# A pre-LN block on one core: weight readiness moved behind the store, weight sums stored sooner, a third fold buffer, and query exponentials stored from the activation engine

## The chip, the cores and the metric

The kernel runs on 1 core of one Trainium2 chip, with all five instruction queues of that core in use: TensorE (PE), VectorE (DVE), ScalarE (ACT), GpSimd (POOL) and the sync engine (SP), which here does nothing but issue DMAs. The metric is device time of one launch in microseconds (us). The kernel before takes 1948.48 us, the median of 3 runs (1946.75 to 1950.21).

## The reference, cut to what matters

One sequence of 2048 tokens, width 1024, 32 heads of 32, feed-forward width 3584, all float32:

```python
h  = x + A(layernorm(x), wqkv, w_phi, wo)
h2 = h + relu(layernorm(h) @ w1) @ w2

def A(x, wqkv, w_phi, wo):
    q, k, v = heads(x @ wqkv)
    pq, pk = q @ w_phi, k @ w_phi                       # per head, 32 x 32
    phi_q = concat(softmax(pq), softmax(-pq))           # 64 features
    phi_k = concat(softmax(pk), softmax(-pk))
    kv, z = phi_k.T @ v, phi_k.sum(over tokens)
    return (phi_q @ kv) / (phi_q @ z + 1e-6) @ wo
```

## The kernel before, in words

Every large product is made of three TensorE passes: both operands are split into a high part and a low part, and `mm3` (lines 180 to 183) issues high x high, high x low and low x high. ACT makes the high part of a weight (line 124), POOL or DVE subtracts to get the low part (line 128).

The work is a list of items. Items 0 to 31 project keys and values of the first 8 token tiles (4 column slices of 8 items), 32 to 47 their queries, 48 to 95 the same for the other 8 tiles; then come attention and the output product, the up projection, the down projection. An item of a projection has 8 steps, each three matmuls with 512 columns. Everything beside it is hung on a step by hand: `when(step, f, ...)` records `f` right after that step of the whole list. So each engine's queue is fixed before the run and is taken strictly in order.

Three kinds of side work matter here.

Folding. The key and query weights are multiplied with `w_phi` on the chip, in eight pieces p of eight blocks k each. `fold_step` issues four small matmuls into one of two PSUM banks named `tp` and copies them with ACT into a tile called `wp0` in the source and `wp` in the profile (lines 288 and 291); two blocks fill one tile. `fold_store` (line 300) has SP write the tile to DRAM (`wpk` for keys, `wpq` for queries) and, in the kernel before, marks the two blocks as usable at once. The weight ring `Units` asks `ready(key)` in every step and, when a block is marked and a raw buffer is free, records its load on SP (line 310 for the key half, 311 for the value half, 314 for a query block). Key slice 0 of the first half never goes through this; `ready` lets slice 0 pass always.

Weight sums. `t_load` has SP bring 512 KB of `w1` or `w2` into one of two tiles `b` (line 337), `t_sum` has POOL form four sums in place (line 347), `t_store` has SP write the result to DRAM (line 350, `t<-b`). There are 56 such rounds, one in ten steps, in the projections. A `t_load` can't start before the store of the round two earlier has landed, since it reuses that tile.

Query exponentials. For each of 32 query items DVE writes a tile `qe` (lines 502 and 503, two tiles in turn), ACT takes the exponential (line 507), and SP writes it to DRAM (line 511, `ed<-qe`), from where attention reads it later. The `when` lines for it are three steps after the exponential's.

```python
298        r = (p - 4) % 2
300        sp.dma_start(dst..., wp_of.pop((p, j))...)          # fold_store: then marks both blocks
1069   when(step + 9 + k, t_sum, j, k)
1070   when(step + 18, t_store, w, p, j)
```

Of the kernel before, what the change touches and what calls it, by code (L numbers as in the profile page):

```python
# [9 lines left out]
F32 = mybir.dt.float32  # L10
# [5 lines left out]
P = 128  # L16
# [123 lines left out]
def kernel(  # L140
# [12 lines left out]
    v, act, pool, pe, sp = nc.vector, nc.scalar, nc.gpsimd, nc.tensor, nc.sync  # L153
# [12 lines left out]
    def tp_bank():  # L166
        return psum.tile([P, 512], F32, name="tp", bufs=2)
# [20 lines left out]
    def do(n, k, f, *args):  # L188
        at[n, k].append((f, args))
# [6 lines left out]
    ed = [dram.tile([P, 8, 4, 256], F32, name=f"ed{b}") for b in range(4)]  # L196
# [65 lines left out]
    fp = folds.enter_context(tc.tile_pool(name="fold", bufs=2))  # L262
# [13 lines left out]
    def fold_mm(p, k, ps):  # L276
        for i in range(2):
            pe.matmul(ps[:, i * P:(i + 1) * P], wt_of[p, i][:, k * P:(k + 1) * P],
                      bd[:, (2 * p + i) % 8, :], start=True, stop=True)

    def fold_step(p, k):
        ps = tp_bank()[:, 0:256]
        fold_mm(p, k, ps)
        if k % 2 == 0:
            wp_of[p, k // 2] = fp.tile([P, 512], F32, name="wp0", bufs=2)
        sb = wp_of[p, k // 2][:, k % 2 * 256:(k % 2 + 1) * 256]
        if p < 4:
            act.activation(sb, ps, AF.Copy)
        else:

            act.activation(sb.rearrange("p (r c f) -> p c r f", r=2, c=4),
                           ps.rearrange("p (c r f) -> p c r f", r=2, c=4), AF.Copy)

    wp_of = {}

    def fold_store(p, j):

        r = (p - 4) % 2
        dst = wpk[p][2 * j:2 * j + 2] if p < 4 else wpq[(p - 4) // 2][2 * j:2 * j + 2, :, r * 256:(r + 1) * 256]
        sp.dma_start(dst.rearrange("k p f -> p k f"), wp_of.pop((p, j)).rearrange("p (k f) -> p k f", k=2))  # L300
        for k in (2 * j, 2 * j + 1):
            if p < 4 or p % 2:
                folded.add(("kv", p, k) if p < 4 else ("q", (p - 4) // 2, k))
# [83 lines left out]
        place[0] = k % 2 == 1  # L387

    def first_copy(j):
        wp_of[0, j] = fp.tile([P, 512], F32, name="wp0", bufs=2)  # L390
        act.activation(wp_of[0, j], first_ps.pop(j), AF.Copy)

    def ready(key):
# [10 lines left out]
    e_of, v_of, phi_of, kv_ps, kd_of = {}, {}, {}, {}, {}  # L404
# [100 lines left out]

    def q_second(s, t):
        act.activation(e_of[s, t], e_of[s, t], AF.Exp)

    def q_store(s, t):
        b, i = place_of[t]  # L510
        sp.dma_start(ed[b][:, 4 * s:4 * s + 4, i, :], e_of[s, t].rearrange("p (a c) s f -> p a (c s f)", a=4))

    def q_third(s, t):
        b, i = place_of[t]
# [312 lines left out]
    def item(gen, *args, keys):  # L827
        items.append((gen, args + (keys,)))
        steps.extend((k,) for k in keys)
        return len(items) - 1  # L830
# [11 lines left out]
    for b, tiles in enumerate(groups):  # L842
        for hf in range(2):

            pairs = b == 0 and hf == 0
            for j in range(0, 4, 2 if pairs else 1):
# [3 lines left out]
                for half in range(2):  # L850
                    n = item(wo_pair, tiles[j:j + 2], hf, half, keys=[("wo", hf, 4 * half + k // 2) for k in range(8)])
# [26 lines left out]
    def when(step, f, *args):  # L878

        if step < 8 * first_up:  # L880
            do(step // 8, step % 8, f, *args)
        else:
            do(first_up + (step - 8 * first_up) // 4, step % 4, f, *args)
# [4 lines left out]
    for t in range(1, NT):  # L888
        n = t - 1 if t < HT else q_n[1, t - HT] + 1
# [20 lines left out]
    for i, j in enumerate((2, 3, 0, 1)):  # L910
        do(1 + i // 2, 2 + 4 * (i % 2), first_copy, j)
        when(8 * (1 + i // 2) + 2 + 4 * (i % 2) + 3, fold_store, 0, j)
    todo = [(p, k) for p in range(1, 8) for k in range(NK)]
    for n in range(1, 32):
        for k in ((6,) if n < 8 and n not in (3, 4, 5) else (2, 6)):
            if not todo:
                break
            p, kk = todo.pop(0)
            do(n, k, fold_step, p, kk)
            if kk % 2:  # L920
                when(8 * n + k + 3, fold_store, p, kk // 2)
            if kk == 2 and p < 7:
                do(n, k, wt_load, p + 1, sp)
    assert not todo
# [71 lines left out]
    a0 = last_kv + 6  # L996
    for (sl, t), n in q_n.items():
        when(8 * n + 14, q_second, sl, t)
        when(8 * n + 17, q_store, sl, t)
        when(8 * n + 19, q_third, sl, t)  # L1000
    for u in range(32):
        start = 8 * (a0 + u) if u >= 8 else 8 * (last_kv + 4) + 19 * u // 2
# [32 lines left out]
    def up_step(b, p, m):  # L1035

        return up0 + 4 * (up_n[b, p, m] + 1 - first_up)

    for j, m in enumerate(UP):

        for g in range(2):
            step = up0 + (8 * j + (-62, -32)[g] if j < 4 else 6 * (j - 4) + 10 + 2 * g)
# [4 lines left out]
            step = up_step(0, NP - 1, m) + 3 * j  # L1047
# [13 lines left out]
    for n, (w, p, j) in enumerate((w, p, j) for w in (1, 2) for p in range(NP) for j in range(2)):  # L1061
        step = 24 + 10 * n
        if step > 8 * q_n[1, 0] - 20:
            step += 64
        when(step, t_load, w, p, j)
        for k in range(4):
            when(step + 9 + k, t_sum, j, k)
        when(step + 18, t_store, w, p, j)

    for b in range(2):  # L1070
        for m in DOWN:
            n = down_n[b, m, NP - 1] + 1
            name, more = {1: "x1", 5: "x4", 6: "x2", 4: "x3"}.get(m), \
# [111 lines left out]
```

## Time and profile before

| | us |
|---|---|
| median of 3 runs | 1948.48 |
| lowest, highest run | 1946.75, 1950.21 |
| the profiled execution's own time | 1954.31 |
| its span in the trace | 1952.5 |
| PE busy in the span | 1911.8 (98%) |
| DVE, POOL, ACT busy | 1027.3, 966.4, 756.0 |
| mean clock granted to PE | 0.993 of full |

The profile is one execution. PE's row of 40 slices reads 9 nearly everywhere; the slices that read lower are the first and the seventh (8) and the third (7). A matmul's busy time includes its pipelined tail, so a busy PE is an upper reading. The DMA row (mean busy share of 16 engines) runs from 5 to 8 tenths.

### The profile page before, as it was taken

Reading aid. Unit: us, or ns where it says so; the run is one execution under the profiler, and the core shown is the slowest. Engines: PE = TensorE matmul, PEld = TensorE weight load, DVE = VectorE, ACT = ScalarE, POOL = GpSimd, SP = SyncE. Lnnn points to the kernel's source line nnn. Section 1 sums busy time; section 2 is a strip of 40 time slices with the busy share of each in tenths; the row PEclk is TensorE's granted clock in tenths of the full one; section 3 lists DMA queues with packets and bytes.
Section 4 is the critical chain, followed back from the end, with each engine's and each line's share of the span. In section 5 each row is a group of like instructions: output and inputs, shape, how many; then the busy total and the mean of one; then the engine's idle time right before and its main releaser. Section 6 shows DMA issues by size and latency. Waiting matters only on the chain.

```text
span 1952.5 us, 31527 instructions
## 1 busy us (share of the span) xinstructions
PE 1911.8 (98%) x11416; PEld 1563.7 (80%) x11416; DVE 1027.3 (53%) x1695; ACT 756.0 (39%) x1374; POOL 966.4 (49%) x935
## 2 busy tenths in 40 slices
PE   8979998999999999999999999999999999999999
PEld 6867887877877777788888888888888888888887
DVE  5646567866759976645454464433443343334333
ACT  5422224422223312135454464444444444444442
POOL 3646672389984788622333322222244444444443
PEclk9999999999999999999999999999999999999999
DMA  5667777556657556788677796665677677876665
GB/s 189 202 219 251 254 248 245 175 183 218 204 190 232 176 192 207 251 273 250 220 247 245 255 309 215 203 196 182 196 248 227 202 220 229 261 216 214 216 215 178
DMA packets 292701, 432.16 MB, mean 221 GB/s; under 512 B 24384, under 2 KB 150336, under 8 KB 292544
## 3 DMA queue, kind: packets, MB, share of 16 engines
q1 hardware_dynamic: 292544, 430.14, 69.7%
q8 instruction: 90, 1.47, 0.3%
q14 instruction: 67, 0.55, 0.1%
HBM read 292.68 MB, written 137.36 MB: 220 GB/s over the span
## 4 chain that ended last, share of the span: by engine, by line
PE 77%; DMA 11%; POOL 6%; DVE 2%; issue 1%; SPq 1%; ACT 1%; POOLq 0%; ACTq 0%; DVEq 0%
PE mm L181 19%; PE mm L182 19%; PE mm L183 19%; DMA t<-b 5%; PE ac L183 4%; PE ac L182 4%; PE ac L181 4%; POOL b L347 3%; PE tp L183 2%; PE tp L181 2%; PE tp L182 2%; DMA b<-in_w_dram 2%; POOL w L128 2%; PE tp L244 1%; POOL zacc L437 1%
## 5 line engine op out<-in xcount | busy, mean ns | idle before, releaser
L128 POOL TENSOR_TENSOR w<-raw,w 128x512 fp32r<-128x512 f32 x355 | 472.6, 1333 | 736.1 <-ACT w L124 694.2
L124 ACT ACTIVATE w<-raw 128x512 fp32r<-128x512 f32 x686 | 408.8, 626 | 500.6 <-PE mm L183 240.2
L128 DVE TENSOR_TENSOR w<-raw,w 128x512 fp32r<-128x512 f32 x331 | 269.2, 814 | 539.2 <-ACT w L124 535.9
L181 PE MATMUL mm<-w,xT 128*128 128x512 f32 x768 | 315.2, 410 | 2.3 <-ACT w L124 2.3
L182 PE MATMUL mm<-w,xT 128*128 128x512 f32 x768 | 303.8, 396 | 8.1 <-POOL w L128 4.6
L183 PE MATMUL mm<-w,xT 128*128 128x512 f32 x768 | 302.4, 394 | 0.0
L181 PE MATMUL mm<-hT,w 128*128 128x512 f32 x672 | 262.6, 391 | 0.0
L183 PE MATMUL mm<-hT,w 128*128 128x512 f32 x672 | 261.6, 389 | 0.0
L182 PE MATMUL mm<-hT,w 128*128 128x512 f32 x672 | 261.5, 389 | 0.0
L347 POOL TENSOR_TENSOR b<-b 128x256 f32<-128x256 f32 x224 | 179.9, 803 | 113.7 <-DMA b<-in_w_dram 100.3
L182 PEld LDWEIGHTS mm<-w,xT 128*128 128x128 f32 x768 | 146.6, 191 | 39.2 <-POOL w L128 7.2
L181 PEld LDWEIGHTS mm<-w,xT 128*128 128x128 f32 x768 | 146.5, 191 | 34.8 <-ACT w L124 2.8
L183 PEld LDWEIGHTS mm<-w,xT 128*128 128x128 f32 x768 | 146.2, 190 | 31.7
L181 PE MATMUL mm<-w 128*128 128x512 f32 x392 | 152.5, 389 | 0.0
L182 PE MATMUL mm<-w 128*128 128x512 f32 x392 | 152.5, 389 | 0.0
L183 PE MATMUL mm<-w 128*128 128x512 f32 x392 | 152.5, 389 | 0.0
L183 PEld LDWEIGHTS mm<-hT,w 128*128 128x128 f32 x672 | 126.1, 188 | 26.2
L182 PEld LDWEIGHTS mm<-hT,w 128*128 128x128 f32 x672 | 126.2, 188 | 25.9
L181 PEld LDWEIGHTS mm<-hT,w 128*128 128x128 f32 x672 | 126.2, 188 | 25.9
L437 POOL TENSOR_TENSOR zacc<-zacc,kphi 128x512 f32<-128x512 f32 x60 | 83.2, 1386 | 5.9 <-DVE kphi L429 5.9
L183 PEld LDWEIGHTS mm<-w 128*128 128x128 f32 x392 | 73.6, 188 | 15.3
L181 PEld LDWEIGHTS mm<-w 128*128 128x128 f32 x392 | 73.6, 188 | 15.3
(161 smaller groups left out, 3142.6 us busy)
## 6 DMA issues: line engine op xcount, KB each, us to landing
raw<-t SPq DMA_DIRECT2D x224, 256.0 KB, 3.9
raw<-ad SPq DMA_DIRECT2D x196, 256.0 KB, 3.0
raw<-in_w_dram SPq DMA_DIRECT2D x168, 256.0 KB, 3.1
b<-in_w_dram SPq DMA_DIRECT2D x56, 512.0 KB, 4.0
t<-b SPq DMA_DIRECT2D x56, 512.0 KB, 4.6
ad<-c SPq DMA_DIRECT2D x112, 256.0 KB, 3.7
ad<-s SPq DMA_DIRECT2D x84, 256.0 KB, 4.1
ed<-qe SPq DMA_DIRECT2D x32, 512.0 KB, 4.5
```

What stands on the lines that cost most here:

```text
L124: nc.scalar.activation(w[:, 0, :], raw[1], AF.Copy)
L128: eng.tensor_tensor(out=w[:, 1, :], in0=raw[1], in1=w[:, 0, :].bitcast(F32), op=ALU.subtract)
L181: pe.matmul(ps, a_hi, b_hi, start=first, stop=False, skip_group_check=more)
L182: pe.matmul(ps, a_hi, b_lo, start=False, stop=False, skip_group_check=more)
L183: pe.matmul(ps, a_lo, b_hi, start=False, stop=last, skip_group_check=more)
L244: pe.transpose(pt[:, k, :], xn[:, (4 * j + k) * P:(4 * j + k + 1) * P], ident)
L347: pool.tensor_tensor(out=tsum[j, *out], in0=tsum[j, *a], in1=tsum[j, *b], op=ALU.subtract)
L437: pool.tensor_tensor(out=zacc[s], in0=zacc[s], in1=phi_of[key], op=ALU.add)
```

## The change

Four edits. The readiness marks leave `fold_store` for a function of their own, `fold_ready`, which the plan calls 8 steps after the store (at step 40 for piece 0). The fold tile has three buffers in place of two. The query exponentials' store moves from SP, three steps after the exponential, to ACT, right behind it. The weight sums are recorded 2 steps sooner, and their store 5 steps sooner.

```diff
@@ fold_step, first_copy
-            wp_of[p, k // 2] = fp.tile([P, 512], F32, name="wp0", bufs=2)
+            wp_of[p, k // 2] = fp.tile([P, 512], F32, name="wp0", bufs=3)
@@ fold_store
         sp.dma_start(dst.rearrange("k p f -> p k f"), wp_of.pop((p, j)).rearrange("p (k f) -> p k f", k=2))
+
+    def fold_ready(p, j):
+
         for k in (2 * j, 2 * j + 1):
             if p < 4 or p % 2:
                 folded.add(("kv", p, k) if p < 4 else ("q", (p - 4) // 2, k))
@@ q_second
         act.activation(e_of[s, t], e_of[s, t], AF.Exp)
-
-    def q_store(s, t):
         b, i = place_of[t]
-        sp.dma_start(ed[b][:, 4 * s:4 * s + 4, i, :], e_of[s, t].rearrange("p (a c) s f -> p a (c s f)", a=4))
+        act.dma_start(ed[b][:, 4 * s:4 * s + 4, i, :], e_of[s, t].rearrange("p (a c) s f -> p a (c s f)", a=4))
@@ the plan
         when(8 * (1 + i // 2) + 2 + 4 * (i % 2) + 3, fold_store, 0, j)
+        when(40, fold_ready, 0, j)
...
                 when(8 * n + k + 3, fold_store, p, kk // 2)
+                when(8 * n + k + 11, fold_ready, p, kk // 2)
...
         when(8 * n + 14, q_second, sl, t)
-        when(8 * n + 17, q_store, sl, t)
...
-            when(step + 9 + k, t_sum, j, k)
-        when(step + 18, t_store, w, p, j)
+            when(step + 7 + k, t_sum, j, k)
+        when(step + 13, t_store, w, p, j)
```

The first place is SP's queue around items 10 to 13 of the kernel before, at about 110 to 127 us; `b` is a tile of weight sums, `wp0` a fold tile, `raw` a raw weight buffer.

```order
L350 DMA t1_2_312<-b_1209 512x1x256
L337 DMA b_1391<-in_w1_dram 128x4x256
L300 DMA wpk2_76<-wp0_1375 128x2x256
L310 DMA raw_1429<-wpk2_76 128x256
L311 DMA raw_1429<-in_wv_dram 128x256
L310 DMA raw_1432<-wpk2_76 128x256
L311 DMA raw_1432<-in_wv_dram 128x256
L350 DMA t1_2_312<-b_1295 512x1x256
L337 DMA b_1477<-in_w1_dram 128x4x256
L214 DMA xin_1495<-in_x_dram 128x1024
L300 DMA wpk3_77<-wp0_1446 128x2x256
```

The same place of the changed kernel, whose lines 313, 314, 340 and 353 are 310, 311, 337 and 350 of the kernel before.

```order
L340 DMA b_1381<-in_w1_dram 128x4x256
L353 DMA t1_2_312<-b_1291 512x1x256
L300 DMA wpk2_76<-wp0_1368 128x2x256
L313 DMA raw_1421<-wpk2_76 128x256
L314 DMA raw_1421<-in_wv_dram 128x256
L313 DMA raw_1424<-wpk2_76 128x256
L314 DMA raw_1424<-in_wv_dram 128x256
L340 DMA b_1473<-in_w1_dram 128x4x256
L214 DMA xin_1490<-in_x_dram 128x1024
L300 DMA wpk3_77<-wp0_1438 128x2x256
L353 DMA t1_3_313<-b_1381 512x1x256
```

Before, each store of sums stands right ahead of the load that needs it landed, and each pair of weight loads is behind the fold store of its own blocks. Now the store of sums stands right behind a load, with five other DMAs between it and the load that needs it, and the four weight loads read the blocks of the fold store one earlier.

The second place is SP's queue in the query items of the first half (300 us in the trace), with the counters that each row waits for. `DMAHW0` to `DMAHW7` are eight completion counters that all DMAs of the program share in turn.

```order
L511 DMA ed1_81<-qe_3146 128x4x256 [waits Activation_49]
L350 DMA t1_12_322<-b_3121 512x1x256 [waits DMAHW3_49,DMAHW1_49,Pool_49]
L337 DMA b_3222<-in_w1_dram 128x4x256 [waits DMAHW2_49,DMAHW1_49]
L511 DMA ed1_81<-qe_3188 128x4x256 [waits Activation_49]
L350 DMA t1_13_323<-b_3171 512x1x256 [waits DMAHW6_49,DMAHW4_49,Pool_49]
L511 DMA ed0_80<-qe_3231 128x4x256 [waits Activation_49]
```

In the changed kernel the query stores stand in ACT's queue, here the same items; line 510 is 507 before, line 512 is 511.

```order
L510 ACTIVATE qe_3148<-qe_3148 128x1024 [waits DMAHW7_49,DVE_49]
L512 DMA ed1_81<-qe_3148 128x4x256 [waits DMAHW0_49,Activation_49]
L510 ACTIVATE qe_3190<-qe_3190 128x1024 [waits DMAHW5_49,DVE_49]
L512 DMA ed1_81<-qe_3190 128x4x256 [waits DMAHW4_49,Activation_49]
L510 ACTIVATE qe_3233<-qe_3233 128x1024 [waits DMAHW0_49,DVE_49]
L512 DMA ed0_80<-qe_3233 128x4x256 [waits DMAHW6_49,Activation_49]
L510 ACTIVATE qe_3272<-qe_3272 128x1024 [waits DMAHW4_49,DVE_49]
L512 DMA ed0_80<-qe_3272 128x4x256 [waits DMAHW7_49,Activation_49]
L124 ACTIVATE w_3316<-raw_2911 128x512 [waits PE_49,Pool_49]
```

Each store now follows its exponential, and SP's rows for them are gone. Most of the moved rows also wait for a DMA counter, and behind the last of them on ACT stand weight splits (line 124).

## Rows read from the trace of the kernel before

**Rows 1.** Waits of PE, whole span: total us, times, longest.

```profile
PE tp L278 <- ACT wp L288: 10.6, 4, 6.1
PE tp L244 <- ACT wp L288: 4.0, 1, 4.0
PE tp L278 <- ACT wp L291: 3.6, 3, 2.7
```

**Rows 2.** Stages: length; busy PE, PEld, DVE, ACT, POOL; granted clock, DMA share, GB/s.

```profile
97.60:146.40 48.80, 38.18 (x267) 30.98 (x266) 20.49 (x45) 10.68 (x28) 21.85 (x27) 0.93 0.69 219
146.40:195.00 48.60, 43.94 (x280) 36.02 (x279) 30.40 (x64) 12.06 (x31) 33.72 (x43) 0.96 0.77 252
293.00:342.00 49.00, 43.53 (x193) 35.30 (x192) 38.13 (x57) 20.31 (x26) 13.57 (x15) 0.93 0.77 246
```

**Rows 3.** Same view, the stretches at half clock that follow these stalls.

```profile
44.80:50.10 5.30, 5.30 (x17) 4.53 (x18) 2.92 (x5) 3.02 (x5) 1.11 (x1) 0.50 0.53 135
132.10:135.40 3.30, 3.10 (x9) 2.67 (x10) 2.93 (x8) 1.22 (x4) 3.03 (x5) 0.50 0.96 340
173.00:176.40 3.40, 3.13 (x9) 2.67 (x10) 2.49 (x6) 1.28 (x4) 1.95 (x3) 0.50 0.85 295
314.20:319.70 5.50, 5.45 (x13) 4.34 (x14) 5.46 (x8) 1.14 (x2) 2.37 (x2) 0.50 0.91 283
```

**Rows 4.** Timeline of ACT, fold copies: start, us, [idle before, released by].

```profile
119.09 0.38 ACT L288 ACTIVATE wp<-tp 128x256 f32<-128x256 f32 x1 [8.68 <-DMA wpk<-wp]
...
131.87 0.38 ACT L288 ACTIVATE wp<-tp 128x256 f32<-128x256 f32 x1 [11.33 <-DMA wpk<-wp]
```

**Rows 5.** Timeline of SP's queue at the same place.

```profile
110.72 0.53 SPq L350 DMA_DIRECT2D t<-b  x1
114.14 0.38 SPq L337 DMA_DIRECT2D b<-in_w_dram  x1
114.62 0.46 SPq L300 DMA_DIRECT2D wpk<-wp  x1
119.05 0.34 SPq L310 DMA_DIRECT2D raw<-wpk  x1
...
120.90 0.53 SPq L350 DMA_DIRECT2D t<-b  x1
```

**Rows 6.** Waits of SP's queue, whole span.

```profile
SPq L337 <- DMA t<-b: 192.1, 49, 8.6
SPq L511 <- ACT qe L507: 45.8, 12, 9.5
SPq L310 <- DMA wpk<-wp: 38.1, 8, 6.5
```

**Rows 7.** Timelines of ACT, SP, DVE and PE, query items.

```profile
293.52 1.06 ACT L507 ACTIVATE qe<-qe 128x1024 f32<-128x1024 f32 x1 [3.07 <-DVE qe L503]
...
302.60 0.50 SPq L511 DMA_DIRECT2D ed<-qe  x1
...
307.61 0.69 DVE L502 TENSOR_TENSOR qe<-mm,qmx 128x512 f32<-128x512 f32 x1 [2.78 <-DMA ed<-qe]
...
309.94 3.21 ACT L124 ACTIVATE w<-raw 128x512 fp32r<-128x512 f32 x6
...
314.25 0.80 PE L182 MATMUL mm<-w,xT 128*128 128x512 f32 x1 [3.14 <-DVE w L128]
```

**Rows 8.** Page: POOL's sums (busy, mean ns, idle before); issues (count, KB, us to landing).

```profile
L347 POOL TENSOR_TENSOR b<-b 128x256 f32<-128x256 f32 x224 | 179.9, 803 | 113.7 <-DMA b<-in_w_dram 100.3
...
t<-b SPq DMA_DIRECT2D x56, 512.0 KB, 4.6
...
ed<-qe SPq DMA_DIRECT2D x32, 512.0 KB, 4.5
```

**Rows 9.** Timeline of PE at full clock, first pass of two steps that follow each other.

```profile
105.96 0.39 PE L181 MATMUL mm<-w,xT 128*128 128x512 f32 x1
...
106.64 0.39 PE L181 MATMUL mm<-w,xT 128*128 128x512 f32 x1
```

More of the change, by code (lines that the diff above doesn't have):

```diff
@@ L389, in first_copy @@
     def first_copy(j):
-        wp_of[0, j] = fp.tile([P, 512], F32, name="wp0", bufs=2)
+        wp_of[0, j] = fp.tile([P, 512], F32, name="wp0", bufs=3)
         act.activation(wp_of[0, j], first_ps.pop(j), AF.Copy)
```

## The prediction, made before the changed kernel ran

> **What bounds the kernel now.** The page comes first: PE is busy 1911.8 of 1952.5 us, so what can be won without taking work from PE is its 40.7 us of idle time, and the time in which it ran at half clock. The list of PE's waits tells whose they are [rows 1]: 18.2 us in eight waits end with an ACT copy of a fold tile (10.6 and 3.6 before the fold matmuls of line 278, 4.0 before a transpose). The table by stage puts most of them between 97 and 195 us [rows 2]; a third stage, 293 to 342 us, has 49.0 - 43.5 = 5.5 us of idle PE of another kind.
>
> Behind the fold stalls stands SP. The ACT copies at 119.1 and 131.9 us waited 8.7 and 11.3 us for a fold store to land [rows 4]: the tile of two pairs earlier was not free. It wasn't free because SP was late [rows 5]. In the round from 110.72 to 120.90 us SP stores sums, stands 3.4 us until that store has landed because the next load of sums reuses the tile, issues a fold store, and stands 4.4 us until that has landed because the next DMA reads it. That is 7.9 us of standing in a round of 10.2. PE needs for the ten steps of a round 10 x 0.68 = 6.8 us, beside transposes and folds [rows 9]. So in this stage SP sets the pace, ACT hangs on SP and PE on ACT. Over the whole span SP stands 192.1 us for stores of sums and 38.1 us for fold stores [rows 6].
>
> In the third stage [rows 7] the exponential of a query tile ends at 294.6, but its store is issued at 302.60, since SP stood at a load of sums. DVE gets the tile at 307.61, the next exponential follows, and behind it in ACT's order six weight splits start at 309.94. PE's matmul that waited for the last of these chains starts at 314.25.
>
> After four of the stalls the clock falls. The granted clock is 0.50 (1.2 GHz, not 2.4) in the stretches that follow them [rows 3], with 5.30 + 3.10 + 3.13 + 5.45 = 17.0 us of busy PE; at full clock this is half, 8.5 us less. If the stalls go, I take it that these go too.
>
> **The change part by part.** *Readiness 8 steps later.* Nothing is computed; the loads stand further back in SP's queue. Eight steps are at least 5.4 us, against 4.4 us of waiting in the row, so the 38.1 us of rows 6 go nearly whole. A load that comes 8 steps later could miss its use. The tightest is the last pair of key slice 1: fold in item 5, marked at step 57, wanted in step 70. That is 13 steps, 8.8 us, for a landing and a split; later slices have 60 steps and more. Price if SP is late by a whole wait of 8.6 us there: one stall of up to 8.6 us. I take 0.
>
> *Sums sooner.* Between a store of sums and the load that needs it now lie 7 steps (4.8 us) where there were 2; the store lands in 4.6 us in the median [rows 8], the longest wait being 8.6. SP's mean wait of 192.1 / 49 = 3.9 us falls to between 0 and 3.9; I take 1. What is added: the store may stand for POOL. The last of four sums is recorded 10 steps after the load and takes 0.80 us, so 7.6 us against 8.8 us for the store. POOL has waited 100.3 us for the loads, 1.8 per round of 56 [rows 8]. If it is that late against the margin of 1.2, SP stands 0.6 us per round and behind it weight loads and fold stores; POOL's own order moves little, since each sum passes at most a weight split or a running total. By these terms SP's round is 10.2 - 4.4 - (3.4 - 1) + 0.6 = 4.0 us, and without any gain from the sums 5.8. Both are under 6.8.
>
> *Third fold tile.* A copy now needs the store of three pairs back. At 131.9 us this is the landing that freed the copy at 119.1, so the 11.3 us of ACT's wait are covered by 12.8. It costs only space. Even where SP keeps its old pace for some rounds this cover holds.
>
> *Query stores on ACT.* 32 issues leave SP and enter ACT. An issue of this size holds SP 0.50 us [rows 7]; 32 x 0.5 = 16 us of ACT, which is busy 20.3 of 49 us there, so it costs nothing unless a weight split is next. The store then starts at 294.6 and, landing in 4.5 us [rows 8], frees its tile at about 299, eight us before DVE got it. With it go the late splits. What is late next is DVE's own order, with 38 of 49 us busy; I add nothing for it. The bounds of this edit: -5.5 with the clock's 2.7, or a loss, below.
>
> The Trainium skill says in "DMA: Bandwidth & Descriptors", section "Issuing engines are not separate DMA queues", that DMAs from any engine run on the same 16 DMA engines, so that issuing from two saves only the sequencer's initiating time. By this rule alone the move would be worth 16 us of SP's time off the path, and the third stall would stay. The rows differ in what they say is late: the store was late by its place behind SP's standing load (8.0 us from exponential to issue) and not in its transfer, so I side with the rows.
>
> **The sum,** against the profiled execution's 1954.3 us: -14.2 and -4.0 (fold waits), -5.5 (query stage), -8.5 (clock) = -32.2. New waits come where PE runs denser. From 97.6 to 195 us 48.8 x 219 + 48.6 x 252 GB/s = 22.9 MB are moved [rows 2]; without 15.3 us of idle time and 3.1 of slow clock that is in 79 us, 290 GB/s, and the DMA share would go from 0.73 to 0.90. Landings will take longer. The cost lies between 0 and half of what this stage gives back, (14.2 + 3.1) / 2 = 8.7 us. I take 4, nearer to the row of rows 5, where SP keeps a margin. Together -28.2: 1926 us for a profiled execution. The median of the runs shown is 5.8 us under the profiled one, so the forecast is 1948.5 - 28.2 = 1920 us.
>
> **The rivals.** *SP or the DMA engines stay the bound* between 97 and 195 us. For: a share of 0.90, and waits of up to 8.6 us for a store of sums, longer than the 4.8 now given. Against: the fold waits go by order alone, and the third tile adds a round of cover. Then half of the stage stays, and the rest of the forecast holds: 1954.3 - 32.2 + 8.7 + 4 less 5.8, so 1929 us; with nothing won there at all, 1938.
>
> *The third stage keeps its stall.* ACT's stores wait for DMA counters too, so a late SP reaches the splits by another way, as the skill's rule would also have it in effect. For: most moved rows name such a counter. Against: each is for a DMA that the plan issues earlier, so it costs only where SP is late. Price 5.5 + 2.7: 1928 us.
>
> *ACT stands for SP: slower.* The eight counters are shared, so a store in ACT's queue waits until an earlier DMA on the same counter has landed, and that one is mostly SP's. If SP is a load of sums behind (8.6 us) whenever a query store comes, ACT stands 8.6 us in front of the splits, 32 times. A split is taken up to 10 steps ahead, 6.8 us of cover, so 1.8 x 32 = 58 us come in place of the gain of 28: 1979 us. It decides from the point where SP is more than 6.8 us late in the query items; up to there it is nothing. Against it: the plan records the last store of sums at step 24 + 64 + 550 + 13 = 651 and the first query store of the second half at 8 x 80 + 14 = 654, so half of the 32 meet no sums, and SP loses its own reasons to be late.
>
> *The change does not do what it says:* the clock falls as before and the waits only change names. Idle time then moves from copies to loads, and 0 to 4 us are won: 1946.
>
> **How the numbers follow.** The forecast 0.58 (1914 to 1926), the bound on SP or a kept third stall 0.25 (1926 to 1939), no change or little 0.09, ACT standing 0.08. What 3 runs can tell from no change is about 0.2%, 3.9 us. From the cases: faster 0.87, same 0.06, slower 0.07. Range 1911 to 1939: below, the new waits at 0 (1916) and 5 us of the 17 (40.7 - 23.7) that no term here takes from PE's idle time; above, all of the stage between 97 and 195 us kept.
>
> **What will show it.** Right: the rows "PE tp L278 <- ACT wp" fall from 14.2 us to under 3; the stages 97 to 195 and 293 to 342 us read 48 or more of 49 busy at clock 1.00; SP's wait for a fold store goes from 38.1 to under 5, for a store of sums from 192 to under 100; DVE's wait for `ed<-qe` is gone. Wrong: ACT rows that wait for a DMA ahead of line 512, SP's rows of line 353 waiting for POOL by tens of us, PE rows that wait for a weight split around item 8, or a new stretch at half clock.

## The result, and the profile after

The changed kernel takes 1916.83 us, the median of 6 runs (1913.62 to 1918.43), against 1950.38 for the kernel before in its 6 runs of the same comparison. The ratio is 0.9829, 95% interval 0.9817 to 0.9842: 33 us faster. The forecast of 1920 (range 1911 to 1939) holds: the time is 3 us under it, the gain 5 us larger than the forecast 28.2.

These are all the waits of PE that are left in the whole span of the changed kernel. The columns are total us, times and longest.

```profile
PE mm L182 <- POOL w L128: 2.9, 4, 1.4
PE tp L1106 <- POOL ones L1102: 1.6, 1, 1.6
PE tp L244 <- ACT xn L237: 1.5, 2, 1.4
PE tp L470 <- DVE kd L463: 1.5, 1, 1.5
PE tp L614 <- issue: 1.1, 2, 0.8
PE mm L182 <- POOL w L388: 0.4, 1, 0.4
```

Every row of [rows 1], 18.2 us in eight waits for an ACT copy, is gone. The stages of [rows 2] read, in the same columns (PE busy first, then the granted clock, the DMA share and GB/s at the end):

```profile
97.60:146.40 48.80, 48.80 (x360) 41.10 (x359) 33.08 (x67) 16.71 (x38) 34.95 (x43) 1.00 0.82 272
146.40:195.00 48.60, 48.60 (x361) 41.00 (x360) 32.89 (x69) 16.08 (x36) 34.10 (x40) 1.00 0.83 280
293.00:342.00 49.00, 49.00 (x242) 40.46 (x241) 43.26 (x70) 26.56 (x37) 11.67 (x12) 1.00 0.63 207
```

PE is never idle there, at full clock. The stages hold more work than before (361 matmuls instead of 280 in the second), since all comes sooner; the DMA engines carry it at a share of 0.82 and 0.83. The four stretches at half clock of [rows 3] are gone, and so is one near 640 us that [rows 3] do not have (first row, kernel before). A new one stands near 530 us (second row, changed kernel), where PE had waited 1.4 us for a weight split on POOL. The columns are length, PE's busy time, granted clock, DMA share and GB/s:

```profile
640.60:644.10 3.50, 3.50 (x29) 0.51 0.20 66
...
529.00:532.40 3.40, 3.40 (x9) 0.50 0.86 236
```

SP's waits that answer to [rows 6] (line 340 is 337 before, 353 is 350):

```profile
SPq L340 <- DMA t<-b: 106.8, 38, 6.3
SPq L353 <- POOL b L350: 59.7, 34, 4.0
...
SPq L300 <- ACT wp L288: 13.9, 8, 4.9
...
SPq L313 <- DMA wpk<-wp: 1.8, 1, 1.8
```

The wait for a store of sums fell from 192.1 to 106.8 us. The sooner store now waits 59.7 us for POOL, where the kernel before had 23.8. The wait of line 313 for a fold store fell from 38.1 us in eight to 1.8 us in one. So SP still stands a good deal, only no longer while others hang on it. SP's queue at the place of [rows 5] shows it:

```profile
104.34 0.71 SPq L300 DMA_DIRECT2D wpk<-wp  x1
105.14 0.61 SPq L353 DMA_DIRECT2D t<-b  x1
105.80 0.74 SPq L214 DMA_DIRECT2D xin<-in_x_dram  x1
111.50 0.37 SPq L300 DMA_DIRECT2D wpk<-wp  x1
114.05 0.37 SPq L340 DMA_DIRECT2D b<-in_w_dram  x1
```

Between the x load and the next fold store SP has 5 us with nothing to issue: the fold store waits for its copy (line 300 for ACT, up to 4.9 us above), not the copy for a store. SP runs ahead of PE.

The stores did not land later with the denser traffic. On the page of the changed kernel, against [rows 8]:

```profile
t<-b SPq DMA_DIRECT2D x56, 512.0 KB, 4.2
...
ed<-qe ACTq DMA_DIRECT2D x32, 512.0 KB, 4.4
```

The loads of folded key weights did land later, in 3.6 us in the median where they had 2.7. The same view of the kernel before, then of the changed kernel:

```profile
raw<-wpk SPq DMA_DIRECT2D x56, 128.0 KB, 2.7
...
raw<-wpk SPq DMA_DIRECT2D x56, 128.0 KB, 3.6
```

The query items, which answer to [rows 7], lie at 255 to 300 us now. ACT's timeline there (an ACTq row is the issue of a DMA):

```profile
258.26 1.06 ACT L510 ACTIVATE qe<-qe 128x1024 f32<-128x1024 f32 x1 [4.38 <-DVE qe L506]
261.75 0.42 ACTq L512 DMA_DIRECT2D ed<-qe  x1
...
280.01 1.06 ACT L510 ACTIVATE qe<-qe 128x1024 f32<-128x1024 f32 x1 [0.60 <-DVE qe L506]
286.09 0.37 ACTq L512 DMA_DIRECT2D ed<-qe  x1
286.63 0.63 ACT L124 ACTIVATE w<-raw 128x512 fp32r<-128x512 f32 x1 [5.56 <-DMA raw<-wpk]
```

The third rival has a true part: ACT stands in front of its stores, 2.4 us at 259.3 and 5.0 us at 281.1, until a DMA issued by SP has landed (the last row names a raw weight). The splits behind it still come nearly in time: from 255 to 300 us PE is busy 44.6 of 45 us.

### The profile page after: what moved, and what is told of

Same layout as the page of the kernel before. It is cut to its first block, busy times and chain, and to the rows that moved or that the text cites. A ratio compares the mean times of both kernels' runs of the same rounds, so it can differ in the third digit from the quotient of the medians.

```text
span 1914.6 us, 31526 instructions
## 1 busy us (share of the span) xinstructions
PE 1901.4 (99%) x11416; PEld 1558.8 (81%) x11416; DVE 1030.4 (54%) x1695; ACT 760.1 (40%) x1374; POOL 967.3 (51%) x935
## 4 chain that ended last, share of the span: by engine, by line
PE 91%; POOL 4%; DMA 2%; issue 1%; DVE 1%; ACT 0%; SPq 0%; POOLq 0%; ACTq 0%; DVEq 0%
PE mm L181 23%; PE mm L182 23%; PE mm L183 23%; PE ac L183 4%; PE ac L181 4%; PE ac L182 4%; PE tp L182 2%; PE tp L181 2%; PE tp L183 2%; POOL b L350 2%; POOL w L128 1%; PE tp L244 1%; PE tp L278 1%; PE tp L614 1%; DMA b<-in_w_dram 1%
## 5 line engine op out<-in xcount | busy, mean ns | idle before, releaser
L182 PEld LDWEIGHTS mm<-w,xT 128*128 128x128 f32 x768 | 144.9, 189 | 34.1 <-POOL w L128 5.9
L181 PEld LDWEIGHTS mm<-w,xT 128*128 128x128 f32 x768 | 144.7, 188 | 31.4 <-issue 2.5
L183 PEld LDWEIGHTS mm<-w,xT 128*128 128x128 f32 x768 | 144.6, 188 | 31.1
L181 PEld LDWEIGHTS mm<-w 128*128 128x128 f32 x392 | 73.6, 188 | 15.3
L182 PEld LDWEIGHTS mm<-w 128*128 128x128 f32 x392 | 73.6, 188 | 15.2
L183 PEld LDWEIGHTS mm<-w 128*128 128x128 f32 x392 | 73.6, 188 | 15.2
```

The source lines that it names most:

```text
L181: pe.matmul(ps, a_hi, b_hi, start=first, stop=False, skip_group_check=more)
L182: pe.matmul(ps, a_hi, b_lo, start=False, stop=False, skip_group_check=more)
L183: pe.matmul(ps, a_lo, b_hi, start=False, stop=last, skip_group_check=more)
```

## The experiments

Eight kernels, each timed beside the kernel before. Four take the changed kernel and undo one edit; four take the kernel before and make one edit.

| kernel | median us | ratio to before | 95% interval |
|---|---|---|---|
| all four edits | 1916.83 | 0.9829 | 0.9817 to 0.9842 |
| all but the third tile | 1922.22 | 0.9853 | 0.9837 to 0.9869 |
| all but the query stores on ACT | 1921.03 | 0.9846 | 0.9831 to 0.9860 |
| all but the sooner sums | 1919.35 | 0.9834 | 0.9820 to 0.9849 |
| all but the later readiness | 1932.66 | 0.9903 | 0.9885 to 0.9920 |
| only the third tile | 1949.02 | 0.9988 | 0.9979 to 0.9997 |
| only the sooner sums | 1941.23 | 0.9942 | 0.9927 to 0.9958 |
| only the query stores on ACT | 1942.00 | 0.9948 | 0.9930 to 0.9966 |
| only the later readiness | 1936.81 | 0.9923 | 0.9907 to 0.9939 |

**Only the third tile.**

```diff
-            wp_of[p, k // 2] = fp.tile([P, 512], F32, name="wp0", bufs=2)
+            wp_of[p, k // 2] = fp.tile([P, 512], F32, name="wp0", bufs=3)
```

> The kernel before with three fold tiles and nothing else. Theory A (SP's pace is the cause, the tile is only cover): SP still stands 7.9 us in each round of sums and fold store, it falls behind by 3.4 us per round, and the third tile absorbs one round's lag (about 7 us) once in each place where the lag has built up. Of the 18.2 us of fold waits some 10 go, with half of their clock loss of 5.8: 1950 - 13 = 1937 us, SP's waits stay near 192 and 38 us, and 'PE <- ACT wp' stays at 5 to 10 us. Theory B (the tile is the cause): all 18.2 and 5.8 go, 1926 us, 'PE <- ACT wp' at most 2 us. Either way the stall in the query items near 300 us stays (5.5 us idle, a stretch at half clock).

It gives 2 us (0.12%), less than either theory expected. PE's waits behind a fold copy are all gone, where theory A let 5 to 10 us of them stay, and others stand in their place (the wait for POOL's splits was 4.6 us before):

```profile
PE mm L182 <- POOL w L128: 9.1, 9, 3.2
PE tp L278 <- DMA wt<-in_wqkT_dram: 5.2, 2, 4.7
PE tp L278 <- DVE xT L178: 3.1, 1, 3.1
```

All of them hang on what SP brings late. Between 55 and 215 us POOL waits 52.3 us for loads of sums, behind which the weight splits stand in its order, and DVE waits 45.0 us for loads of x; the weights to be folded (`wt`) are a load of SP's too. SP's queue there is as before.

```profile
110.21 0.52 SPq L350 DMA_DIRECT2D t<-b  x1
113.66 0.38 SPq L337 DMA_DIRECT2D b<-in_w_dram  x1
114.14 0.46 SPq L300 DMA_DIRECT2D wpk<-wp  x1
118.89 0.34 SPq L310 DMA_DIRECT2D raw<-wpk  x1
...
120.75 0.53 SPq L350 DMA_DIRECT2D t<-b  x1
```

A round still takes 10.5 us, with 3.5 and 4.8 us from each store to the DMA behind it. The early stall, before 48.8 us, is gone, though. PE's row for that stage, kernel before and then this one, in the columns length, busy time, granted clock, DMA share and GB/s:

```profile
0.00:48.80 48.80, 39.47 (x212) 0.94 0.59 189
...
0.00:48.80 48.80, 44.81 (x249) 1.00 0.61 191
```

Over the span PE is idle 1948.1 - 1915.0 = 33.1 us, 7.6 less than before. But it is busy 3.2 us longer (1915.0 against 1911.8): six stretches at half clock instead of five, one of them from 207 to 214 us. So the tile was not the cause (theory B falls), and theory A was wrong on one point: of what the tile's cover gives, most is lost again while SP is late, since PE meets the same lateness at the next thing that SP brings.

**All but the third tile.** The changed kernel with `bufs=2` in both places.

> The changed kernel with two fold tiles. Theory A (SP's pace): SP has kept up, a copy now has 9 steps (6.1 us or more) from its store's place to its need against a landing of 4 to 6 us, so 0 to 5 us come back: 1917 to 1922 us, ACT waits for fold stores in a few copies by 1 to 3 us each. Theory B (the tile): most of the 18.2 us and of their clock loss come back, 1937 to 1941 us.

By the medians 5 us come back, at the upper end of theory A; the intervals just overlap. The trace says where: between 97 and 195 us PE is busy throughout, and one wait of [rows 1], the early one, is back with a stretch at half clock behind it.

```profile
PE tp L244 <- ACT wp L288: 4.2, 1, 4.2
```

So beside a punctual SP the third tile pays for the early stall, and there alone. That wait is in all five kernels with two tiles (4.0 to 4.6 us) and in none of the five with three, whatever their other edits.

**All but the query stores on ACT.**

```diff
+    def q_store(s, t):
+        b, i = place_of[t]
-        act.dma_start(ed[b]...)
+        sp.dma_start(ed[b]...)
...
+        when(8 * n + 17, q_store, sl, t)
```

> The changed kernel with the query exponentials' store back on SP, three steps after the exponential. Theory A (SP was late because of the sums' stores, not because of the queue a store stands in): with sums stored sooner SP stands 2 to 3 us at a time, a store leaves in time, PE loses 0 to 2 us more than in the changed kernel: 1917 to 1919 us. Theory C (it needed the place behind the exponential in ACT's queue): the stall near 300 us is back with 5.5 us of idle PE and 2.7 of slow clock: 1925 us.

By the medians 4 us come back, between the two theories; the intervals overlap. The place shows the old chain, shorter. PE's waits for a split on DVE in the whole span, then SP's queue, then ACT's timeline:

```profile
PE mm L182 <- DVE w L128: 3.6, 2, 3.0
```

```profile
262.63 0.37 SPq L340 DMA_DIRECT2D b<-in_w_dram  x1
...
265.92 0.90 SPq L514 DMA_DIRECT2D ed<-qe  x1
```

```profile
259.47 1.07 ACT L510 ACTIVATE qe<-qe 128x1024 f32<-128x1024 f32 x1 [10.52 <-DVE qe L506]
...
273.43 1.06 ACT L510 ACTIVATE qe<-qe 128x1024 f32<-128x1024 f32 x1 [7.01 <-DVE qe L506]
...
278.24 3.22 ACT L124 ACTIVATE w<-raw 128x512 fp32r<-128x512 f32 x6
```

The exponential that ended at 260.5 has its store issued at 265.92, the one after next runs at 273.43, and six splits follow late at 278.24. PE waits 3.6 us for such splits in all. Theory A is right that a less late SP makes this stall smaller, theory C that it doesn't remove it.

**All but the sooner sums.** The changed kernel with `step + 9 + k` and `step + 18` again.

> The changed kernel with the sums and their store recorded as before (9 and 18 steps). Theory A with its two parts (fold waits 4.4 us and sums' waits 3.4 us of a round of 10.2): the readiness alone brings SP's round to 5.8 us and the third tile covers the rest, so PE loses 0 to 4 us: 1917 to 1921 us, SP's wait for sums' stores back at 170 to 190 us. Theory D (the sums' store is what held SP): the stalls between 97 and 195 us come back in good part, 8 us or more: 1925 to 1935 us.

Theory A holds: 1919.35 can't be told from the changed kernel. SP waits as before for its stores of sums (197.3 us, a little over the 190 expected), and one stage shows what that costs now, 5 us of idle PE behind POOL's splits and a clock of 0.96.

```profile
SPq L340 <- DMA t<-b: 197.3, 51, 8.4
```

```profile
146.40:195.00 48.60, 43.54 (x296) 36.03 (x295) 28.76 (x59) 13.74 (x32) 33.87 (x42) 0.96 0.77 247
```

**All but the later readiness.** The changed kernel with `when(8 * n + k + 3, fold_ready, ...)`; the four marks of piece 0 stay at step 40.

> The changed kernel with the readiness marks back at the place of the store (blocks usable at once). Theory A (SP's pace, each of its waits counts): SP stands again for the landing of each fold store of key slices 1 to 3, 4 to 6 us in some eight places, its round between 97 and 140 us is again over what PE needs, and the third tile covers only the first of it: 5 to 10 us come back, 1922 to 1927 us. Theory E (the sums' store and the tile are enough): 1917 to 1919 us, although SP's wait for fold stores is back near 38 us.

16 us come back by the medians (0.74%), more than theory A expected, and theory E falls. SP stands for fold stores as before the change; the one shown holds the queue 6.0 us:

```profile
SPq L313 <- DMA wpk<-wp: 42.8, 8, 6.4
```

```profile
110.81 0.57 SPq L300 DMA_DIRECT2D wpk<-wp  x1
116.86 0.34 SPq L313 DMA_DIRECT2D raw<-wpk  x1
```

PE's stall is not at the fold copies here either, with three tiles: it waits for splits on POOL (5.5 us of its waits between 60 and 150 us) and for `wt` (2.8).

**Only the sooner sums.** The kernel before with `step + 7 + k` and `step + 13`.

> The kernel before with the weight sums recorded 2 and their store 5 steps sooner, nothing else. Theory A: SP's round falls by some 2.4 us of 10.2 and stays over 6.8, so the fold stalls between 97 and 195 us shrink by half and the early stall and the one in the query items shrink a little: 1938 to 1943 us, SP's wait for sums' stores 100 to 130 us. Theory E (this is the main edit): 1928 to 1933 us.

1941.23 us, in theory A's range; theory E falls. SP's wait for stores of sums falls to 112.0, the one for fold stores stays at 41.0, and PE's waits at line 278 for a fold copy shrink from 14.2 to 4.8 us.

```profile
SPq L337 <- DMA t<-b: 112.0, 38, 5.9
...
SPq L310 <- DMA wpk<-wp: 41.0, 8, 6.7
```

**Only the query stores on ACT.** The kernel before with the store behind the exponential, on ACT.

> The kernel before with the query exponentials' store on ACT and nothing else: SP is late here. Theory C (the place in SP's queue was the cause of the stall near 300 us): its 5.5 us of idle PE and 2.7 of slow clock go, 1942 us, fold stalls unchanged. Theory F (ACT then stands for a late SP, by the shared completion counters): rows of ACT that wait for DMAs issued by SP appear at the stores, with 10 us or more in the first half's query items, the stall stays or grows: 1950 to 1960 us.

1942.00 us, theory C's number. SP stands 191.7 us for sums as before, and the stage of the stall is nearly without idle time (columns as in [rows 2]).

```profile
293.00:342.00 49.00, 48.88 (x235) 40.05 (x234) 39.41 (x62) 24.66 (x32) 13.09 (x13) 1.00 0.73 236
```

ACT's timeline in that stage shows what its store does to it:

```profile
307.93 1.06 ACT L507 ACTIVATE qe<-qe 128x1024 f32<-128x1024 f32 x1 [0.64 <-DVE qe L503]
313.61 0.37 ACTq L509 DMA_DIRECT2D ed<-qe  x1
314.43 0.63 ACT L124 ACTIVATE w<-raw 128x512 fp32r<-128x512 f32 x1 [5.43 <-DMA raw<-wpk]
```

The exponential ends at 309.0 and the store is issued at 313.61: ACT stands 4.6 us for a landing of SP's late queue, and PE still has its operands. Theory F falls. The gain is 2 us above the 8.2 of theory C's sum. A second stall went with this edit: PE's wait at line 613 of the kernel before (1.6 us at the longest, put down to no engine), which stands ahead of the half clock near 640 us. A wait of 1.6 us there is in all five kernels with the query stores on SP, and the longest is 0.9 us in the five with them on ACT. Why the store's place matters there stays open.

**Only the later readiness.** The kernel before with `fold_ready` and its two `when` lines.

> The kernel before with the readiness marks 8 steps later, nothing else (two tiles, sums as before, query stores on SP). Theory A: SP's round loses its 4.4 us of waiting for fold stores and comes to 5.8, under what PE needs, so most of the 14.2 us of fold waits and 3 of their clock loss between 97 and 195 us go; the early stall (4.0 and 2.7) and the one in the query items (5.5 and 2.7) stay: 1933 to 1938 us. Theory E: readiness is the small part, 1944 to 1950 us.

1936.81 us, theory A's number: one edit gives 15 of the 33 us. The stage that was worst is full (first row), although the sums wait as before and there are two tiles. The next one is not (second row): PE waits 3.7 us there for a fold copy.

```profile
97.60:146.40 48.80, 48.80 (x335) 41.17 (x333) 29.78 (x62) 15.48 (x36) 35.00 (x41) 1.00 0.76 249
146.40:195.00 48.60, 44.91 (x332) 37.57 (x332) 29.11 (x62) 14.79 (x35) 31.43 (x40) 0.96 0.76 250
```

Taken by the ratios, the four single edits give 0.12 + 0.58 + 0.52 + 0.77 = 1.99%, all together 1.71%, and undone one by one they cost 0.24 + 0.17 + 0.05 + 0.74 = 1.20%. They overlap: once SP keeps up, the next edit that speeds it up finds less to win.

## Why the prediction was right, point by point

*What bounds the kernel.* Shown for the worse of the two stages: taking out only the wait for fold stores fills 97 to 146 us, and giving the copies another tile does not (PE busy 40.8 of 48.8 us with the tile alone). From 146 to 195 us it takes more than that one edit.

*Fold waits, -18.2 us.* They came to 0, as the sum had it. Of its two reasons the readiness is shown to be the main one, and the tile is what the early 4.0 us need. The sentence that the third tile's cover holds even where SP keeps its old pace is right by the letter, since no copy is waited for in the kernel with the tile alone; but it was counted as time won, and that kernel won 2 us, because the wait went to `wt` loads and splits. The total was not touched, since SP did not keep its pace.

*Query stage, -5.5 us.* Right: in the kernel with only this edit PE's idle time in the stage fell from 5.5 to 0.1 us. By the Trainium skill, "DMA: Bandwidth & Descriptors", section "Issuing engines are not separate DMA queues", issuing from a second engine saves only the sequencer's time to initiate the DMAs. By that alone the stall would have stayed; it went, so here the measurement decides against reading the rule as the whole gain. What the move changed was the store's place behind a standing queue.

*Clock, -8.5 us.* Right, and that it is met to the tenth is luck. The four stretches of [rows 3] went, a fifth near 640 us that the sum had not counted went too, and a new one came near 530 us. In busy time at half clock this is 17.0 + 3.5 - 3.4 = 17.1 us, of which half is 8.5. PE's busy time fell by more, from 1911.8 to 1901.4 us with the same 11416 matmuls; the other 1.9 us lie in no such stretch, and where they come from is open.

*New waits, +4 us.* This is the term that was mis-sized: it is not there. The estimate of a DMA share of 0.90 was near (0.82 and 0.83), and some landings did take longer (3.6 against 2.7 us for a load of folded keys, while a store of sums took 4.2 against 4.6). The wrong step is that this reaches PE. PE's idle time fell from 40.7 to 1914.6 - 1901.4 = 13.2 us, by 27.5 us, where the sum had 23.7 - 4 = 19.7. Of the 7.8 us between them 4 are this term and 3.8 are waits that no term took, of which the range allowed 5.

*The total.* Trace against trace the gain is 1952.5 - 1914.6 = 37.9 us, and the sum had 28.2; the 9.7 us between them are the 4, the 3.8 and the 1.9 above. The medians are 33.5 us apart, because the profiled execution of the kernel before lay 3.9 us above its median in the comparison and that of the changed kernel 0.5 below. The forecast also started from 1948.5 us, where the kernel before took 1950.4 in the comparison. So that 1920 came within 3 us is in part luck: the sum was short by 5 us against the medians and by 9.7 against the traces.

*Sums sooner, SP's round.* SP's mean wait was forecast at 1 us per round and is 106.8 / 56 = 1.9; that for POOL at 0.6 per round and is 59.7 / 56 = 1.1. Both were too small, and neither mattered. With them the forecast's sum for SP's round gives 10.2 - 4.4 - (3.4 - 1.9) + 1.1 = 5.4 us. PE's side of that comparison was off as well: 6.8 us is ten steps without transposes and folds. In the 48.8 us from 97.6 of the changed kernel, where PE is never idle, 58 steps begin:

```profile
L181 PE MATMUL mm<-w,xT 128*128 128x512 f32 x58 | 23.9, 412 | 0.0
```

So ten steps take 8.4 us there. By these rows, as an estimate, the SP of the kernel before, with 10.2 us in the round shown, was late by 1.8 us per round and not by the 3.4 that the expectation for the tile alone counts with.

*The signs written down.* Not all came as written. PE's waits for fold copies, the busy time and clock of the stages and SP's wait for fold stores did. SP's wait for stores of sums went to 106.8 us and not under 100, and two waits of DVE for a query store are left (2.3 us, from 23.1). Three of the signs for wrong came: ACT stands ahead of line 512, line 353 waits tens of us for POOL, and there is a new stretch at half clock. The forecast held all the same, since the first two are waits of queues that PE did not hang on, and the third cost 1.7 us. As signs they were ill chosen.

*The rivals.* The bound on SP or the DMA engines did not come. ACT stood for SP up to 5.0 us, less than the 6.8 from which it would decide; the kernel with only this edit, where SP was late, shows that it did not reach that point there either (its ACT row at a split waits 5.4 us for a DMA at the most). That waits only change names is not what the whole change did, but it is what most of the third tile alone did.

## What to carry to other kernels

Ask of an in-order DMA queue what stands behind each DMA that waits: here a load placed right behind the store it reads, or a load right behind the store that frees its buffer, held up everything else in the queue for a landing. Moving the dependent DMA some steps back, past work that does not wait, gained nearly half of all that was won here, and no cost showed. More buffers for one client of a late queue handed most of the wait to the next client (2 us won, where 18.2 us of waits had gone): mend the queue first, then see which buffer is still short.

## What the runs showed of the hardware that was not expected

With the DMA engines at 0.82 to 0.83 busy and 272 to 280 GB/s in the two stages from 97 to 195 us, where they had been at 0.69 to 0.77 and 219 to 252 GB/s, landings did not all move one way. Stores landed no later (4.2 us against 4.6 for the 512 KB stores of sums, 4.4 against 4.5 for those of query tiles), 128 KB loads of folded keys did (3.6 against 2.7); these are medians over the whole span. And a DMA issued by ACT can hold ACT for a transfer of SP's, up to 5.0 us here, while its issue alone takes 0.37 to 0.42 us.
